# Two FFT convolutions: the transposes between the stages moved from TensorE and PSUM copies to crossbar DMA

## The chip, the cores and the metric

The kernel runs on one core of one Trainium2 chip. The metric is device time in microseconds (us), the median of several executions; lower is better. A run that is over 1.5% above the fastest of its kernel counts as slow here. A ratio below one means faster than the kernel before. Every ratio is the mean time of one kernel's fast runs over the mean time of the kernel before in the same rounds on the same chip, so it is not quite the ratio of the medians quoted beside it. The bracket after a ratio is its 95% interval.

Engine names in the profile: PE is TensorE's matmuls, PEld its weight loads, DVE is VectorE, ACT is ScalarE, POOL is GpSimd, SPq is the DMA queue that SyncE issues. L222 is a source line. Line numbers differ between kernels because the edits shift them.

## The reference, cut to what matters

Four residual layers over a sequence of 2048 rows by 512 features, in bfloat16:

```python
x = A_u
x = x + A(layernorm(x))   # long convolution, by FFT
x = x + B(layernorm(x))   # dilated sliding attention, window 8, 32 heads
x = x + A(layernorm(x))   # the same convolution kernel again
x = x + B(layernorm(x))

def A(u):                 # cut
    K  = einsum("dn,dnl,dn->dl", Cc, exp(logdA * l), dB).real   # kernel of 2048 taps per feature
    Yf = rfft(pad(u)) * rfft(pad(K))
    return irfft(Yf)[:L] + u * Dskip
```

The first layer must also make K, from tables of powers, and its spectrum. The third layer re-uses the spectrum, which the first has stored in DRAM.

## The kernel before

An FFT of each block of features has two stages, each a matmul with constants. Stage 1 (`s1`) gives `Z`, stage 2 (`s2`) needs `Z` with its two axes exchanged, `zt`. In the kernel before, TensorE transposes eight 128x128 blocks into PSUM and VectorE or ScalarE copies them out.

```python
def s2(self, Z, cs, dsts, what):                 # cut
    def turn(i):
        pt = self.psT.tile([128, 2, 4, 128], BF, name="pt", tag="psT")
        for r in range(2):
            for g in range(4):
                nc.tensor.transpose(pt[:, r, g, :], Z[:, r, i * 4 + g, :], ident[:])
        zt = self.w.tile([128, 2, 512], BF, name="zt", tag="zt")
        self.evac("zt_" + what, zt[:]..., pt[:]...)
        zts[i] = zt
    turn(0)
    for i in range(cs):
        if i + 1 < cs:
            turn(i + 1)
        zt = zts.pop(i)
        xp = self.pst([128, 2, 512])             # from the pool psA
        ... four matmuls with C2, then self.evac(what, dsts[i], xp[:])
```

PSUM holds two pools in the first convolution: `psA`, two buffers of 4 KB per partition for every matmul result, and `psT`, two buffers of 2 KB for the transposes.

```python
psT = es.enter_context(tc.tile_pool(name="k_psT", bufs=2, space=PSUM))
psA = es.enter_context(tc.tile_pool(name="k_psA", bufs=2, space=PSUM))
cv = Conv(nc, tc, es, C, X, psA, psT, ("zt_xc",))
```

The first convolution works on four blocks of 128 features while VectorE makes the tables for the next ones (`Xtab`, `Ytab`, `Y2tab`). After the last table comes an end that has no tables left to fill gaps: two halves of a last 64 features (u = 0, 1) get their spectrum, a product, an inverse and the final matmuls. Their spectra have a function of their own. It uses `psT` for the transposes and for the results `xpu`.

```python
def spectrum32(self, KT, drow, dst, ps):         # cut: stage 1 into psu, copied to Z by two engines
    pt = self.psT.tile([128, 2, 4, 128], BF, name="pt", tag="psT")
    zt = self.w.tile([128, 2, 512], BF, name="zt", tag="zt")
    ... eight transposes, two copies
    for r, (a, b) in ((0, (0, 2)), (1, (1, 0))):
        xp = self.psT.tile([128, 512], F32, name="xpu", tag="psT")
        nc.tensor.matmul(xp[:], C2[:, a, :], zt[:, 0, :], start=True, stop=False)
        nc.tensor.matmul(xp[:], C2[:, b, :], zt[:, 1, :], start=False, stop=True)
        (nc.scalar.copy if r == 0 else nc.vector.tensor_copy)(dst[:, r, :], xp[:])
```

The second convolution is a software pipeline over 16 chunks, with a lag for each stage:

```python
for k in range(16 + 13):
    for fn, lag in ((final, 13), (inverse, 8), (product, 7), (s2, 6), (turn, 5), (s1, 0)):
        if 0 <= k - lag < 16:
            fn(k - lag)
```

A build step orders each engine's instructions by the program's order, its priorities and the free buffers. The order is then fixed, and an instruction that is ready can stand behind one that waits; a case, at 247.47 us, is shown below.

## Time and profile before

608.52 us, median of 3 runs (607.86 to 608.82).

The first line is the page's part 1: busy time, share of the span, instructions. After it comes the table of stretches for the middle of the first convolution (72 to 115 and 115 to 233.4 us), its end (233.4 to 268) and the second convolution (398 to 468): length, busy time of each engine, the granted clock of TensorE as a share, the share of DMA time, GB/s.

```profile
PE 445.1 (73%) x5743; PEld 289.0 (48%) x5786; DVE 514.4 (85%) x976; ACT 338.9 (56%) x465; POOL 12.7 (2%) x50
...
72.00:115.00 43.00, 30.98 (x737) 21.24 (x741) 41.14 (x75) 25.30 (x27) 0.83 (x6) 0.91 0.08 26
115.00:233.40 118.40, 85.36 (x1805) 63.44 (x1814) 112.03 (x212) 65.15 (x81) 0.72 (x6) 0.89 0.21 64
233.40:268.00 34.60, 22.81 (x362) 16.35 (x364) 27.37 (x88) 19.49 (x31) 6.06 (x1) 0.80 0.34 107
398.00:468.00 70.00, 57.35 (x571) 42.52 (x576) 63.06 (x141) 49.17 (x66) 0.00 (x0) 0.95 0.00 1
```

VectorE is busy 41.1 of 43 us and 112.0 of 118.4 us in the middle of the first convolution, and 63.1 of 70 us in the second: it sets the time there. At the end of the first convolution it is busy 27.4 of 34.6 us only; a chain through all engines runs there.

The next lines are VectorE's timeline in the second convolution: start, duration, engine and line, what it wrote from what. One period of the pipeline:

```profile
410.54 0.68 DVE L726 TENSOR_TENSOR pa<-xc,Kt 128x1024 bf16<-128x1024 bf16 x1
411.14 0.68 DVE L727 TENSOR_TENSOR pb<-xc,Kt 128x1024 bf16<-128x1024 bf16 x1
411.74 0.69 DVE L708 COPY zt<-pt 128x1024 bf16<-128x1024 bf16 x1
412.34 0.68 DVE L749 CAST VT<-vp 128x512 bf16<-128x512 f32 x1
412.94 0.42 DVE L728 TENSOR_TENSOR Y<-pa,pb 128x512 bf16<-128x512 bf16 x1
413.27 0.42 DVE L729 TENSOR_TENSOR Y<-pa,pb 128x512 bf16<-128x512 bf16 x1
413.61 0.69 DVE L726 TENSOR_TENSOR pa<-xc,Kt 128x1024 bf16<-128x1024 bf16 x1
```

From `pa` to the next `pa` is 3.07 us with no gap. The `zt` copy takes 0.60 us of it from start to start (its duration of 0.69 overlaps the next instruction). It is what the change would remove.

### The profile page before, as it was taken

Reading aid. Unit: us, or ns where it says so; the run is one execution under the profiler, and the core shown is the slowest. Engines: PE = TensorE matmul, PEld = TensorE weight load, DVE = VectorE, ACT = ScalarE, POOL = GpSimd, SP = SyncE. Lnnn points to the kernel's source line nnn. Section 1 sums busy time; section 2 is a strip of 40 time slices with the busy share of each in tenths; the row PEclk is TensorE's granted clock in tenths of the full one; section 3 lists DMA queues with packets and bytes.
Section 4 is the critical chain, followed back from the end, with each engine's and each line's share of the span. In section 5 each row is a group of like instructions: output and inputs, shape, how many; then the busy total and the mean of one; then the engine's idle time right before and its main releaser. Section 6 shows DMA issues by size and latency. Waiting matters only on the chain.

```text
span 606.0 us, 13365 instructions
## 1 busy us (share of the span) xinstructions
PE 445.1 (73%) x5743; PEld 289.0 (48%) x5786; DVE 514.4 (85%) x976; ACT 338.9 (56%) x465; POOL 12.7 (2%) x50
## 2 busy tenths in 40 slices
PE   1101776876767776679987779978995899858996
PEld 0100554564554565454332766656764433327763
DVE  5999799998998999775977899859999588689950
ACT  4999357555662755646574223467973556722144
POOL 0000000000000000400000000000000000000000
PEclk9999989898996897869998599989998799968999
DMA  9101001221131023600004060000000000040011
GB/s 291 67 1 35 19 20 37 87 56 36 41 103 37 3 106 72 209 1 1 2 1 118 4 264 16 2 0 1 3 1 0 2 2 0 1 121 1 1 72 69
DMA packets 24346, 28.78 MB, mean 47 GB/s; under 512 B 15074, under 2 KB 20067, under 8 KB 23007
## 3 DMA queue, kind: packets, MB, share of 16 engines
q1 hardware_dynamic: 22702, 27.54, 13.8%
q8 instruction: 45, 0.74, 0.5%
q10 hardware_dynamic: 1584, 0.39, 0.3%
q14 instruction: 15, 0.11, 0.1%
HBM read 15.89 MB, written 8.39 MB: 40 GB/s over the span
## 4 chain that ended last, share of the span: by engine, by line
DVE 52%; PE 28%; ACT 9%; issue 8%; DMA 2%; POOL 0%; SPq 0%; POOLq 0%; ACTq 0%; DVEq 0%
PE ps_qk L829 7%; DVE prod L931 6%; DVE ta L479 4%; DVE Y2tab L518 4%; DVE tb L480 4%; DVE Ytab L516 4%; PE ps_o L955 4%; PE ps_v L843 3%; DVE Xtab L481 3%; DVE ln_st_b L150 3%; PE Lp L875 2%; DVE Ytab L481 2%; PE po L946 2%; DVE ln_st_a L150 2%; DVE pa L726 2%
## 5 line engine op out<-in xcount | busy, mean ns | idle before, releaser
L946 PE MATMUL po<-sb_ident,prod 128*128 128x128 bf16 x1024 | 72.7, 232 | 11.4 <-DVE prod L931 7.9
L946 PEld LDWEIGHTS <-prod 128*128 128x128 bf16 x1024 | 65.2, 105 | 20.6 <-DVE prod L931 17.2
L829 PE MATMUL ps_qk<-xnT,wqk 128*128 128x512 bf16 x245 | 63.7, 391 | 4.3 <-ACT xnT L814 1.2
L862 DVE TENSOR_TENSOR prod<-qT,kT 128x2048 bf16<-128x2048 bf16 (+3 forms) x48 | 43.2, 953 | 14.0 <-ACT qT L831 7.2
L931 DVE TENSOR_TENSOR prod<-V,L 128x2048 bf16<-128x2048 bf16 (+3 forms) x48 | 43.6, 947 | 6.4 <-PE po L946 6.4
L949 ACT CAST oT<-po 128x1024 bf16<-128x1024 f32 x16 | 15.4, 1015 | 56.6 <-PE po L946 56.6
L195 PE MATMUL psA<-X,sb_F 128*128 128x128 bf16 x128 | 14.9, 236 | 36.2 <-ACT X L578 32.3
L870 DVE TENSOR_TENSOR prod<-qT,kT 128x2048 bf16<-128x2048 bf16 (+3 forms) x40 | 34.9, 902 | 6.9 <-ACT kT L831 4.3
L829 PEld LDWEIGHTS <-wqk 128*128 128x128 bf16 x256 | 23.5, 100 | 32.5 <-issue 12.2
L195 PEld LDWEIGHTS <-sb_F 128*128 128x128 bf16 x256 | 16.6, 100 | 45.6 <-issue 42.8
L535 PE MATMUL psk<-Ytab,Xtab 128*32 128x64 bf16 x1024 | 26.1, 214 | 15.6 <-DVE Xtab L481 5.8
L955 PE MATMUL ps_o<-wo_t,oT 128*128 128x512 bf16 x121 | 33.5, 380 | 4.7 <-ACT oT L949 3.9
L931 DVE TENSOR_TENSOR prod<-Vp,L 128x2048 bf16<-128x2048 bf16 (+3 forms) x40 | 34.9, 896 | 0.0
L182 ACT CAST Z<-psA 128x1024 bf16<-128x1024 f32 (+1 forms) x32 | 28.8, 974 | 9.6 <-PE psA L195 9.5
L875 PE MATMUL Lp<-prod,sb_bones 128*32 128x512 bf16 x256 | 25.4, 416 | 9.6 <-DVE prod L870 4.9
L538 PE MATMUL psk<-Y2tab,Xtab 128*32 128x48 bf16 x1024 | 24.8, 211 | 9.8 <-issue 7.3
L535 PEld LDWEIGHTS <-Xtab 128*32 128x32 bf16 x1024 | 22.7, 113 | 17.9 <-issue 15.2
L516 DVE TENSOR_TENSOR Ytab<-Ytab,MA 128x2048 bf16<-128x2048 bf16 (+1 forms) x33 | 30.6, 929 | 0.2
L518 DVE TENSOR_TENSOR Y2tab<-Ytab,MB 128x2048 bf16<-128x2048 bf16 (+1 forms) x33 | 30.6, 927 | 0.0
L843 PE MATMUL ps_v<-wv,xnT 128*128 128x512 bf16 x126 | 28.2, 379 | 1.8 <-ACT V L845 1.7
L538 PEld LDWEIGHTS <-Xtab 128*32 128x32 bf16 x1024 | 22.2, 106 | 13.0 <-issue 11.8
L150 DVE BATCH_NORM_STATS2 ln_st_b<-X 128x6 f32<-128x384 bf16 (+2 forms) x80 | 23.5, 357 | 3.8 <-ACT X L308 3.8
(195 smaller groups left out, 1100.0 us busy)
## 6 DMA issues: line engine op xcount, KB each, us to landing
kt_scratch<-Kt SPq DMA_DIRECT2D x4, 1024.0 KB, 4.3
Kt<-kt_scratch SPq DMA_DIRECT2D x4, 1024.0 KB, 7.2
Vp<-V SPq DMA_DIRECT2D x2, 1568.0 KB, 9.1
X<-in_A_u_dram SPq DMA_DIRECT2D x4, 512.0 KB, 5.6
Xr<-in_A_u_dram SPq DMA_DIRECT2D x4, 512.0 KB, 4.6
out_dram<-X SPq DMA_DIRECT2D x4, 512.0 KB, 2.6
k_scratch<-KTq SPq DMA_DIRECT2D x7, 256.0 KB, 2.0
KT<-k_scratch SPq DMA_DIRECT2D x7, 256.0 KB, 3.5
```

The source lines that it names most:

```text
L150: self.nc.vector.bn_stats(self.st[:, j, part, :], X[:, j, a:b])
L516: nc.vector.tensor_tensor(v(Y[:, :, :, q * EYB:(q + 1) * EYB, :]), src, vm(self.mult(self.MA, lev, hc, EYB)), ALU.mult)
L518: nc.vector.tensor_tensor(v(Y2[:, :, :, (q - 1) * EYB:q * EYB, :]), src, vm(self.mult(self.MB, lev, hc, EYB)), ALU.mult)
L535: nc.tensor.matmul(psk[32 * g:32 * g + 32, ds, :], xs, Y[:, m // 2, h, :, t], start=(m == 0), stop=False, skip_group_check=True)
L538: nc.tensor.matmul(psk[32 * g:32 * g + 32, ds, EYB:], xs, Y2[:, 1 - m // 2, h, :, t], start=False, stop=(m == 3), skip_group_check=True)
L829: nc.tensor.matmul(ps[:], wqk[:, ct, f0:f0 + 128], xnT[:, ct, s0:s0 + 512], start=(ct == 0), stop=(ct == 3))
L843: nc.tensor.matmul(ps[:].rearrange("p a b -> p (a b)"), xnT[:, ct, j * 128:(j + 1) * 128], wv[:, ct, :], start=(ct == 0), stop=(ct == 3))
L862: nc.vector.tensor_tensor(pr[:, :, (ja - j0) * 128:(ja - j0) * 128 + n], qT[fp][:, :, ja * 128: ja * 128 + n], kT[fp][:, :, (ja - sh) * 12 ...
L875: nc.tensor.matmul(Lp[r0:r0 + 32, w // 4, :], bones[:, w % 4, :], pr[:, f2, hb * 512:(hb + 1) * 512], start=(w % 4 == 0), stop=(w % 4 == 3 ...
L931: nc.vector.tensor_tensor(p2[:, ja - j0: ja - j0 + n, :].rearrange("p j (t d h) -> p (j t) d h", t=2, d=DH), src.rearrange("p j (t d h) -> ...
L946: nc.tensor.matmul(po[f2][:, jj, :], p2[:, jj, f2 * 128:(f2 + 1) * 128], ident[:], start=(w == 0 and jj % 4 == 0), stop=(w == W - 1), skip ...
L955: nc.tensor.matmul(ps[:], oT[:, ft, j * 128:(j + 1) * 128], wo_t[:, ft, :], start=(ft == 0), stop=False)
```

## The change

The intent: take 384 transposes from TensorE and their copies from VectorE and ScalarE, and let the DMA crossbar do them from SBUF to SBUF, in 46 transfers of 256 KB and 4 of 128 KB. The PSUM of `psT` becomes a third `psA` buffer (a fourth in the second convolution). The Trainium skill, page "DMA: Bandwidth & Descriptors", section "DMA Transpose (X-bar)", says that plain transfers of this kind are issued from the Sync or Scalar queue only, and, under its heading on two transposing streams, that two streams in flight together can corrupt each other. The change puts all of them on one queue.

```diff
+def turn(nc, zt, Z, g0, n):
+    for r in range(2):
+        nc.sync.dma_start_transpose(zt[:, r, 0:n * 128].rearrange("q (g k) -> q g k", k=128),
+                                    Z[:, r, g0:g0 + n, :].rearrange("k g q -> k (g q)"))
 ... in s2:
-        def turn(i):  (transposes into psT, copy out)
+        for i0 in range(0, cs, 2):
+            zt = self.w.tile([128, 2, 1024], BF, name="zt", tag="zt")
+            turn(nc, zt, Z, i0 * 4, 8)
+            for i in range(2):
+                zts[i0 + i] = zt[:, :, i * 512:i * 512 + 512]
 ... in spectrum32:
-        pt = self.psT.tile(...)  (transposes, two copies)
+        zt = self.w.tile([128, 2, 1024], BF, name="zt", tag="zt")
+        turn(nc, zt, Z, 0, 4)
+        xp = self.pst([128, 2, 512])
         for r, (a, b) in ((0, (0, 2)), (1, (1, 0))):
-            xp = self.psT.tile([128, 512], F32, name="xpu", tag="psT")
-            ... matmuls into xp[:]
+            ... matmuls into xp[:, r, :], copied out by ScalarE (r = 0) and VectorE (r = 1)
 ... first convolution:
-        psT = es.enter_context(tc.tile_pool(name="k_psT", bufs=2, space=PSUM))
-        psA = es.enter_context(tc.tile_pool(name="k_psA", bufs=2, space=PSUM))
+        psA = es.enter_context(tc.tile_pool(name="k_psA", bufs=3, space=PSUM))
 ... second convolution:
-        psA ... bufs=3   psT ... bufs=2
+        tp = es.enter_context(tc.tile_pool(name="a_zt", bufs=2))
+        psA ... bufs=4
-        def turn(k):   (eight transposes, VectorE copy)
+        def turns(k):
+            if k % 2 == 0:
+                t = tp.tile([128, 2, 1024], BF, name="zt", tag="zt")
+                turn(nc, t, Z[k // 4], (k % 4) * 4, 8)
+                zt[k], zt[k + 1] = t[:, :, 0:512], t[:, :, 512:1024]
```

To make room in SBUF, one constant (`bones`) and one set of statistics are also allocated later; that moves a small load and is left aside.

More of the change, by code (lines that the diff above doesn't have):

```diff
@@ L90, in make_consts @@
     fc = _fft_consts()
-    bones_np = np.zeros((128, 4, 32), dtype=np.float32)
-    for f in range(128):
-        for k in range(4):
-            bones_np[f, k, 8 * k + f // 16] = 1.0
     for name in ("F1", "F1T"):
@@ L97, in make_consts @@
     todo = [("ident", _bf(np.eye(128)), BF), ("C2", _bf(fc["C2"]), BF), ("IC", _bf(fc["IC"]), BF),
-            ("bones", _bf(bones_np), BF), ("onesr", _bf(np.ones((1, 128))), BF)]
+            ("onesr", _bf(np.ones((1, 128))), BF)]
     for i, (name, arr, dt) in enumerate(todo):
@@ L117, in load_x, with load_b_weights @@
     return X
-def load_b_weights(nc, const, wqkv, wo):
+def load_b_weights(nc, const, C, wqkv, wo):
+    bones_np = np.zeros((128, 4, 32), dtype=np.float32)
+    for f in range(128):
+        for k in range(4):
+            bones_np[f, k, 8 * k + f // 16] = 1.0
+    C["bones"] = const.tile([128, 4, 32], BF, name="sb_bones")
     wqk = const.tile([128, 4, 1024], BF, name="wqk")
@@ L130, in load_b_weights @@
         nc.sync.dma_start(wo_t[:, ft, :], src)
+    nc.sync.dma_start(C["bones"][:], nc.inline_tensor(_bf(bones_np), name="c_bones").ap())
     Vp = const.tile([128, 2, NJ - 2, 256], BF, name="Vp")
@@ L161, in norm, with __init__ @@
         self.nc.vector.tensor_scalar(dst, src, self.rstd[:, j:j + 1], self.nb[:, j:j + 1], ALU.mult, ALU.add)
+def turn(nc, zt, Z, g0, n):
+    for r in range(2):
+        nc.sync.dma_start_transpose(zt[:, r, 0:n * 128].rearrange("q (g k) -> q g k", k=128),
+                                    Z[:, r, g0:g0 + n, :].rearrange("k g q -> k (g q)"))
 class Conv:
-    def __init__(self, nc, tc, es, C, X, psA, psT, on_dve, zbufs=2, pbufs=2, vbufs=1):
-        self.nc, self.C, self.X, self.psA, self.psT, self.on_dve = nc, C, X, psA, psT, on_dve
+    def __init__(self, nc, tc, es, C, X, psA, on_dve, zbufs=2, pbufs=2, vbufs=1):
+        self.nc, self.C, self.X, self.psA, self.on_dve = nc, C, X, psA, on_dve
         self.vbufs = vbufs
@@ L201, in s2 @@
     def s2(self, Z, cs, dsts, what):
-        nc, ident, C2 = self.nc, self.C["ident"], self.C["C2"]
+        nc, C2 = self.nc, self.C["C2"]
         zts = {}
-        def turn(i):
-            pt = self.psT.tile([128, 2, 4, 128], BF, name="pt", tag="psT")
-            for r in range(2):
-                for g in range(4):
-                    nc.tensor.transpose(pt[:, r, g, :], Z[:, r, i * 4 + g, :], ident[:])
-            zt = self.w.tile([128, 2, 512], BF, name="zt", tag="zt")
-            self.evac("zt_" + what, zt[:].rearrange("q r k -> q (r k)"), pt[:].rearrange("q r g k -> q (r g k)"))
-            zts[i] = zt
-        turn(0)
+        for i0 in range(0, cs, 2):
[3 more added lines that the diff above has]
+                zts[i0 + i] = zt[:, :, i * 512:i * 512 + 512]
         for i in range(cs):
-            if i + 1 < cs:
-                turn(i + 1)
             zt = zts.pop(i)
@@ L313, in spectrum32 @@
     def spectrum32(self, KT, drow, dst, ps):
-        nc, F1, C2, ident = self.nc, self.C["F1"], self.C["C2"], self.C["ident"]
+        nc, F1, C2 = self.nc, self.C["F1"], self.C["C2"]
         Z = self.z.tile([128, 2, 16, 128], BF, name="Z", tag="Z")
@@ L326, in spectrum32 @@
             (nc.scalar.copy if jh == 0 else nc.vector.tensor_copy)(Z[:, :, 0:4, sl], ps[:, :, :, sl])
-        pt = self.psT.tile([128, 2, 4, 128], BF, name="pt", tag="psT")
-        zt = self.w.tile([128, 2, 512], BF, name="zt", tag="zt")
-        for r in range(2):
-            for g in range(4):
-                nc.tensor.transpose(pt[:, r, g, :], Z[:, r, g, :], ident[:])
-            (nc.vector.tensor_copy if r == 0 else nc.scalar.copy)(zt[:, r, :], pt[:, r].rearrange("q g k -> q (g k)"))
+        zt = self.w.tile([128, 2, 1024], BF, name="zt", tag="zt")
+        turn(nc, zt, Z, 0, 4)
+        xp = self.pst([128, 2, 512])
         for r, (a, b) in ((0, (0, 2)), (1, (1, 0))):
-            xp = self.psT.tile([128, 512], F32, name="xpu", tag="psT")
-            nc.tensor.matmul(xp[:], C2[:, a, :], zt[:, 0, :], start=True, stop=False)
-            nc.tensor.matmul(xp[:], C2[:, b, :], zt[:, 1, :], start=False, stop=True)
-            (nc.scalar.copy if r == 0 else nc.vector.tensor_copy)(dst[:, r, :], xp[:])
+            nc.tensor.matmul(xp[:, r, :], C2[:, a, :], zt[:, 0, 0:512], start=True, stop=False)
+            nc.tensor.matmul(xp[:, r, :], C2[:, b, :], zt[:, 1, 0:512], start=False, stop=True)
+            (nc.scalar.copy if r == 0 else nc.vector.tensor_copy)(dst[:, r, :], xp[:, r, :])
 def load_params(nc, pp, prm):
@@ L580, in kernel_and_first_conv @@
             ladder(nc, pp, pst, identf, raw, MA, MB, cb, nu, fill)
-        psT = es.enter_context(tc.tile_pool(name="k_psT", bufs=2, space=PSUM))
-        psA = es.enter_context(tc.tile_pool(name="k_psA", bufs=2, space=PSUM))
-        cv = Conv(nc, tc, es, C, X, psA, psT, ("zt_xc",))
+        psA = es.enter_context(tc.tile_pool(name="k_psA", bufs=3, space=PSUM))
+        cv = Conv(nc, tc, es, C, X, psA, ())
         kp = es.enter_context(tc.tile_pool(name="k_kt", bufs=1))
@@ L677, in a_layer @@
         wk = es.enter_context(tc.tile_pool(name="a_wk", bufs=3))
-        psA = es.enter_context(tc.tile_pool(name="a_psA", bufs=3, space=PSUM))
-        psT = es.enter_context(tc.tile_pool(name="a_psT", bufs=2, space=PSUM))
+        tp = es.enter_context(tc.tile_pool(name="a_zt", bufs=2))
+        psA = es.enter_context(tc.tile_pool(name="a_psA", bufs=4, space=PSUM))
         ident, C2, IC, F1, F1T = C["ident"], C["C2"], C["IC"], C["F1"], C["F1T"]
@@ L699, in s1 @@
             nc.scalar.copy(Z[dc][:, :, :, q * 32:(q + 1) * 32], ps[:])
-        def turn(k):
-            dc, c = k // 4, k % 4
-            pt = psT.tile([128, 2, 4, 128], BF, name="pt", tag="psT")
-            for r in range(2):
-                for g in range(4):
-                    nc.tensor.transpose(pt[:, r, g, :], Z[dc][:, r, c * 4 + g, :], ident[:])
-            zt[k] = wk.tile([128, 2, 512], BF, name="zt", tag="zt")
-            nc.vector.tensor_copy(zt[k][:].rearrange("q r k -> q (r k)"), pt[:].rearrange("q r g k -> q (r g k)"))
+        def turns(k):
[3 more added lines that the diff above has]
+                zt[k], zt[k + 1] = t[:, :, 0:512], t[:, :, 512:1024]
         def s2(k):
@@ L768, in a_layer @@
         for k in range(16 + 13):
-            for fn, lag in ((final, 13), (inverse, 8), (product, 7), (s2, 6), (turn, 5), (s1, 0)):
+            for fn, lag in ((final, 13), (inverse, 8), (product, 7), (s2, 6), (turns, 5), (s1, 0)):
                 if 0 <= k - lag < 16:
@@ L1011 @@
     ln_b = LnStats(nc, const, [(0, 3 * DCH), (3 * DCH, D - 64), (D - 64, D)], "b", eps)
-    ln_b2 = LnStats(nc, const, [(0, 3 * DCH), (3 * DCH, D)], "b2", eps)
     X, marks = kernel_and_first_conv(nc, tc, C, prm, A_u[0], const, kt_dram, kscr, ln, ln_b)
     const2 = ctx.enter_context(tc.tile_pool(name="const2", bufs=1))
-    Wt, Vp = load_b_weights(nc, const2, B_wqkv, B_wo)
+    ln_b2 = LnStats(nc, const2, [(0, 3 * DCH), (3 * DCH, D)], "b2", eps)
+    Wt, Vp = load_b_weights(nc, const2, C, B_wqkv, B_wo)
     marks = b_layer(nc, tc, C, X, Wt, Vp, ln_b, marks, ln_next=ln)
```

## The prediction

> **What bounds the kernel now.** The page shows VectorE busy 85% of a 606.0 us span, and 52% of the chain that ended last. Both convolutions are bound by VectorE. First convolution with the kernel tables (45 to 266 us): in the table of stretches VectorE is busy 95 to 98% of most 25 us slices up to 190 us, TensorE 60 to 80%. Second convolution (398 to 467 us): in the chain, in order of time, VectorE runs a period of 3.06 us per block: pa 0.60, pb 0.60, the zt copy 0.60, VT 0.60, Y 0.33 twice.
>
> **What goes.** TensorE: 384 transposes, about 0.11 us apart when streamed, some 42 us. VectorE: zt copies 16 x 0.684 us (first) and 16 x 0.682 us (second), in sequence about 0.60 us each, so 9.6 to 11 us per convolution, plus two 0.42 us copies. ScalarE: 14 copies of 1.02 us, mostly off the path. The freed PSUM gives the matmuls one buffer more.
>
> **What comes.** 46 transposing DMAs of 256 KB and 4 of 128 KB, all in order on one queue: 30 full ones in the first convolution, 16 in the second. The trace has none such. Plain 256 KB loads land 3.2 us after issue; 512 KB in 256-byte pieces 4.5 us. The Trainium skill, page "DMA: Bandwidth & Descriptors", section "Latency and other measured facts", gives 261 GB/s for a transposing DMA with a non-contiguous middle dimension; the page "VectorE: DVE Perf Modes", section "The three transpose paths", gives 1309 ns for one 128x128 block. These bracket 1.0 us to 10 us for eight blocks. My estimate, from the first figure and the plain loads: 2.5 us of queue time and 4.5 us to landing.
>
> **On the critical path.**
> - First convolution, 72 to 200 us: the copies stand in VectorE's own sequence, so about 10 us go; the forward transforms have slack, but TensorE, in order, will sometimes stand at a late zt. Net -7 us.
> - Its end, 197 to 262 us: transposes of the last spectra (243 to 250 us) stand in a chain with little filler; a DMA landing replaces about 1.5 us of transposes and copy. Net +4 us.
> - Second convolution: first product 3 us later; then 16 periods shrink from 3.06 to about 2.6 us (VectorE 2.46; ScalarE about 2.6 where Z, xc and VT overlap). If a DMA takes over 2.5 us of queue time, the DMAs set the period instead. Net -3 us.
> - Attention layers: unchanged.
>
> Sum -6 us less some 1.5 us for waits in the DMA queue: **604 us**, 8 in 10 between **588** and **650**. Chances: faster by over 2% **0.27**, within 2% **0.40**, slower by over 2% **0.33**.
>
> **What would show it.** VectorE busy falls from 514 to about 492 us, TensorE from 445 to about 405, ScalarE from 339 to about 324. The DMA issues show zt<-Z, 256 KB, landing in 3 to 6 us. The second convolution's period is about 2.6 us; its first product comes about 3 us later after the first stage. "TensorE matmul psA/xp waits for DMA zt" appears among the waits, below 20 us in all. The end of the first convolution lengthens.
>
> **What would make it wrong.** Slower: a transposing DMA holds the queue for over 4 us each (16 of them are then over 64 us in a 60 us stage, and 30 of them over 120 us), so both convolutions become bound by DMA; or transposes queue behind stores that wait for ScalarE (the queue already waits 128 us for KTq). Faster: landings of about 3 us, always hidden, give -16 us or better, near 590.

## More of the kernel before

VectorE's waits in the end of the first convolution (233 to 265 us): what waited, on what, us in total, times, the longest.

```profile
DVE ln_st_b L150 <- ACT X L308: 3.8, 2, 2.5
DVE VT L277 <- ACT VT L275: 1.5, 1, 1.5
DVE Z L326 <- PE psu L322: 1.3, 1, 1.3
DVE Kt L337 <- PE xpu L336: 0.4, 1, 0.4
```

These are 7.0 us in all, by adding the four.

## The result, and the profile after

607.41 us, median of 4 runs (605.50 to 607.84); the kernel before 608.67 us, median of 4. The ratio is 0.9976 [0.9952, 0.9999]: the same within 2%, a gain of 0.24% where the prediction had 0.75% (4.5 us of 608.5). The result is correct.

The same views as before: part 1, and the table of stretches.

```profile
PE 422.6 (70%) x5362; PEld 261.7 (43%) x5402; DVE 497.0 (82%) x942; ACT 323.0 (53%) x449; POOL 12.9 (2%) x50
...
72.00:115.00 43.00, 26.79 (x613) 15.84 (x617) 38.50 (x68) 18.25 (x19) 0.68 (x4) 0.70 0.59 98
115.00:233.40 118.40, 78.65 (x1821) 55.94 (x1828) 111.96 (x211) 59.46 (x76) 0.70 (x6) 0.86 0.50 104
233.40:268.00 34.60, 19.77 (x179) 11.30 (x177) 15.73 (x56) 14.67 (x24) 6.06 (x1) 0.65 0.45 118
398.00:468.00 70.00, 55.69 (x476) 37.72 (x480) 57.85 (x132) 50.69 (x72) 0.00 (x0) 0.93 0.31 61
```

VectorE lost 17.4 us of work, TensorE 22.5, ScalarE 15.9. In the third stretch VectorE, ScalarE and TensorE are less busy than before. Part of this is only that the end now starts 8 us earlier. Measured from the last table to the first transposes of attention (233.4 to 264.8 us before, 225.1 to 268.3 after), VectorE has the same work, 24.2 and 23.8 us, in 31.4 and in 43.2 us. That is where to look.

To see it, follow milestones through the timelines. Both profiled executions have a span of 606.0 us, so the stages must cancel. The differences in the last column are subtractions.

| stage, from one milestone to the next | before | after | difference |
|---|---|---|---|
| start to the last `Y2tab` instruction (middle of the first convolution) | 233.4 | 225.1 | -8.3 |
| to the first transpose `pt_x` of attention 1 (end of the first convolution) | 31.4 | 43.2 | +11.8 |
| to the first copy of Z in the second convolution (attention 1) | 133.0 | 135.0 | +2.0 |
| to the first normalised row `xn` of attention 2 (second convolution) | 69.6 | 65.0 | -4.6 |
| to the end (attention 2) | 138.6 | 137.7 | -0.9 |

These are single executions; runs of one kernel here differ by up to about 7 us (`e9_tail_dma_pools` below, 592.90 to 600.16), so a difference of one or two microseconds in one row proves nothing.

The transfers, in the view of the tile `zt`: the time that the issuing instruction held its queue (least, median and most, in ns) and the time from issue to landing.

```profile
L169 SPq DMA_TRANSPOSE zt<-Z x50: 1189/1308/2332, 69.7 to 444.9; - x50
...
  DMA zt<-Z: 24.2, 13
...
DMA to landing us min/median/max: 2.5/3.3/6.2
```

One transfer holds the queue 1.31 us and lands after 3.3 us; the prediction had 2.5 and 4.5. TensorE waited 24.2 us for `zt` in all, in 13 places. The same view puts 19.3 us of it (14.4 and 4.9) on stage-2 matmuls of the first convolution, where VectorE sets the time and TensorE has slack.

One period of the second convolution on VectorE:

```profile
430.69 0.69 DVE L719 TENSOR_TENSOR pa<-xc,Kt 128x1024 bf16<-128x1024 bf16 x1
431.30 0.68 DVE L720 TENSOR_TENSOR pb<-xc,Kt 128x1024 bf16<-128x1024 bf16 x1
432.02 0.42 DVE L721 TENSOR_TENSOR Y<-pa,pb 128x512 bf16<-128x512 bf16 x1
432.37 0.42 DVE L722 TENSOR_TENSOR Y<-pa,pb 128x512 bf16<-128x512 bf16 x1
432.70 0.69 DVE L742 CAST VT<-vp 128x512 bf16<-128x512 f32 x1
433.73 0.69 DVE L719 TENSOR_TENSOR pa<-xc,Kt 128x1024 bf16<-128x1024 bf16 x1 [0.35 <-ACT xc L711]
```

The `zt` copy is gone. The period shown is 3.04 us, not 2.47; 0.35 us of the difference is a wait for ScalarE's `xc`, the rest lies in small gaps between starts. It is the longest of the 15 but for the last: their median is 2.66 us (3.15 before) and their mean 2.80 (3.23 before). ScalarE is near its own limit there: its timeline has `xc`, `Z`, `X` and `VT` back to back in 2.85 us (432.69 to 435.54). From the first `pa` to the first `xn` it is 53.2 us instead of 59.4 (from the two timelines), 0.39 us per chunk. What it pays is at the start: the first product waits 8.8 us in place of 1.6.

VectorE's waits at the end of the first convolution (225 to 268 us):

```profile
DVE ln_st_b L152 <- ACT X L309: 8.6, 2, 7.3
DVE Z L327 <- issue: 3.0, 1, 3.0
DVE pa L266 <- ACT Kt L334: 2.4, 1, 2.4
DVE VT L278 <- ACT VT L276: 2.4, 1, 2.4
DVE pa L266 <- ACT Kt L191: 1.6, 1, 1.6
DVE y L285 <- PE psA L292: 0.8, 1, 0.8
DVE Kt L334 <- PE psA L333: 0.4, 1, 0.4
```

They add up to 19.2 us, 12.2 more than before, and so account for the +11.8. The largest wait is for ScalarE's final result X. TensorE's timeline of these microseconds shows what stands behind it (the bracket is the idle time before the instruction and what ended it):

```profile
232.87 0.19 PE L323 MATMUL psu<-KTu,sb_F 128*128 128x32 bf16 x1 [4.37 <-DMA KTu<-k_scratch]
...
246.75 0.39 PE L305 MATMUL psA<-VT,sb_F1T 128*128 128x64 bf16 x8 [1.16 <-ACT VT L276]
...
247.44 0.19 PE L305 MATMUL psA<-VT,sb_F1T 128*128 128x64 bf16 x1
247.47 0.38 PE L332 MATMUL psA<-zt,sb_C 128*128 128x512 bf16 x1
247.68 0.38 PE L333 MATMUL psA<-zt,sb_C 128*128 128x512 bf16 x1
...
251.70 0.38 PE L332 MATMUL psA<-zt,sb_C 128*128 128x512 bf16 x1 [2.98 <-ACT Kt L334]
```

L332 is the first matmul of the last spectrum. Its transposes were issued at 236.63 us and the queue was done with them at 239.13; with the median landing they were there by about 241 (estimate: the second was issued near 237.9, plus the 3.3 us above). But in TensorE's fixed order L332 stands behind inverse and final matmuls (L305) of an earlier part, and starts at 247.47, 14.6 us after the spectrum's first matmul `psu` at 232.87. In the kernel before the first one on record came 7.9 us after it (238.5 to 246.41). A smaller part of the +11.8 lies before `psu`: from the last table to `psu` it is 7.8 us, 5.1 before, and TensorE stands 4.37 us of it at the fetch of `KTu` (the first line above), for which it did not stand before. From `psu` to `pt_x` it is 35.4 us, 26.3 before. Then the second half of the same PSUM tile waits 2.98 us for the copy of the first. ScalarE, meanwhile, stands at two copies of a weight, `wv`, whose load was issued behind the transposes; the chain of waits (start, us on the chain, engine) passes through it:

```profile
243.88 4.60 DMA wvn<-in_B_wqkv_dram
248.57 2.11 ACT wv L831 x2
250.68 0.49 ACT X L309
251.34 0.38 DVE ln_st_b L152 x3
```

### The profile page after: what moved, and what is told of

The parts are those of the page before. It is cut to its first block, busy times and chain, and to the rows that moved or that the text cites. A ratio compares the mean times of both kernels' runs of the same rounds, so it can differ in the third digit from the quotient of the medians.

```text
span 606.0 us, 12631 instructions
## 1 busy us (share of the span) xinstructions
PE 422.6 (70%) x5362; PEld 261.7 (43%) x5402; DVE 497.0 (82%) x942; ACT 323.0 (53%) x449; POOL 12.9 (2%) x50
## 4 chain that ended last, share of the span: by engine, by line
PE 27%; DVE 21%; ACT 9%; issue 7%; DMA 2%; POOL 0%; SPq 0%; POOLq 0%; ACTq 0%
PE ps_qk L822 7%; DVE prod L924 6%; PE ps_o L948 4%; PE ps_v L836 3%; PE Lp L868 2%; PE pt_x L802 2%; PE po L939 2%; DVE prod L863 1%; DVE ln_st_b L152 1%; ACT xc L711 1%; DVE pa L719 1%; DMA zt<-Z 1%; DVE pb L720 1%; ACT oT L942 1%; PE ps_o L950 1%
## 5 line engine op out<-in xcount | busy, mean ns | idle before, releaser
L939 PE MATMUL po<-sb_ident,prod 128*128 128x128 bf16 x1024 | 70.4, 227 | 13.7 <-DVE prod L924 10.3
L939 PEld LDWEIGHTS <-prod 128*128 128x128 bf16 x1024 | 62.3, 102 | 23.5 <-DVE prod L924 20.1
L855 DVE TENSOR_TENSOR prod<-qT,kT 128x2048 bf16<-128x2048 bf16 (+3 forms) x48 | 43.2, 953 | 14.0 <-ACT qT L824 7.2
L822 PEld LDWEIGHTS <-wqk 128*128 128x128 bf16 x256 | 23.4, 100 | 32.1 <-issue 11.8
L204 PEld LDWEIGHTS <-sb_F 128*128 128x128 bf16 x256 | 17.4, 106 | 42.6 <-issue 40.0
L532 PE MATMUL psk<-Ytab,Xtab 128*32 128x64 bf16 x1024 | 23.7, 206 | 12.9 <-DVE Ytab L513 5.6
L535 PE MATMUL psk<-Y2tab,Xtab 128*32 128x48 bf16 x1024 | 22.8, 202 | 13.5 <-issue 12.2
L868 PE MATMUL Lp<-prod,sb_bones 128*32 128x512 bf16 x256 | 24.9, 410 | 10.1 <-DVE prod L863 5.1
L532 PEld LDWEIGHTS <-Xtab 128*32 128x32 bf16 x1024 | 20.9, 105 | 17.8 <-issue 15.5
L222 PE MATMUL psA<-zt,sb_C 128*128 128x512 bf16 x30 | 15.6, 548 | 18.6 <-DMA zt<-Z 14.4
```

Source lines behind the costliest of these rows:

```text
L204: nc.tensor.matmul(o, F1[:, j, r, :], rhs_j(j), start=True, stop=not dk)
L532: nc.tensor.matmul(psk[32 * g:32 * g + 32, ds, :], xs, Y[:, m // 2, h, :, t], start=(m == 0), stop=False, skip_group_check=True)
L822: nc.tensor.matmul(ps[:], wqk[:, ct, f0:f0 + 128], xnT[:, ct, s0:s0 + 512], start=(ct == 0), stop=(ct == 3))
L855: nc.vector.tensor_tensor(pr[:, :, (ja - j0) * 128:(ja - j0) * 128 + n], qT[fp][:, :, ja * 128: ja * 128 + n], kT[fp][:, :, (ja - sh) * 12 ...
L868: nc.tensor.matmul(Lp[r0:r0 + 32, w // 4, :], bones[:, w % 4, :], pr[:, f2, hb * 512:(hb + 1) * 512], start=(w % 4 == 0), stop=(w % 4 == 3 ...
L939: nc.tensor.matmul(po[f2][:, jj, :], p2[:, jj, f2 * 128:(f2 + 1) * 128], ident[:], start=(w == 0 and jj % 4 == 0), stop=(w == W - 1), skip ...
```

## The experiments

Four theories for the +11.8 us at the end:

- **D, the DMA itself**: a landing of about 3.3 us twice, in a chain with no filler, where TensorE and a copy needed some 1.5 us by the prediction's count.
- **P, PSUM**: the change also moved the spectrum's results from a pool of their own (`psT`) into the pool that inverse and final matmuls use. The wait is for a free buffer and for the order that follows, not for the transpose.
- **H, the half tile**: only the one tile of two halves matters, whose second half waits for the copy of the first.
- **L, the loads**: the weights of attention are late behind the transposes in the same queue, and ScalarE stands at `wv`.

All outputs are right.

### Each convolution alone

`e1_conv2_only` keeps the kernel before in the first convolution; `e2_conv1_only` keeps it in the second.

```diff
 e1_conv2_only, against the change
-        psA ... bufs=3;  s2 and spectrum32 by turn() on the DMA
+        psT ... bufs=2, psA ... bufs=2;  s2 and spectrum32 by nc.tensor.transpose and copies
 e2_conv1_only, against the change
-        for fn, lag in (..., (turns, 5), (s1, 0)):       # DMA, psA bufs=4
+        for fn, lag in (..., (turn, 5), (s1, 0)):        # TensorE and VectorE, psA bufs=3, psT bufs=2
```

> Only the second convolution uses the transposing DMA; the first is as in the kernel before (the loads of the weights still moved as in the change). In the two traces the stretch from the end of the first attention layer's last output matmul to the first transposes of the second attention layer shrinks by about 4 us. Theory (the second convolution gains, the end of the first one loses what its middle gains): about 604.5 us, 4 us below the kernel before (ratio 0.993). Rival (both convolutions gain little, the DMA eats its own gain everywhere): 608 us, ratio 0.999.

> Only the first convolution uses the transposing DMA. Theory: its middle gains 8 us, its end loses 12 us, so it is about 3 to 4 us slower than the kernel before: 612 us, ratio 1.006. Rival: the two effects cancel everywhere, ratio 0.999.

Measured: `e1_conv2_only` 605.00 us, ratio 0.9947 [0.9929, 0.9965]; `e2_conv1_only` 613.59 us, ratio 1.0085 [1.0066, 1.0104]; the kernel before 607.75 us (11 runs). The second convolution is a gain of about 0.5% by itself, and the first a loss of about 0.9%. In the trace of `e2_conv1_only` the end of the first convolution is again long, 225.4 to 268.8 us. The two effects do not add up to the change: multiplied, the ratios give 1.0032, and the change measured 0.9976. About 3 us of this sum have no explanation here.

### The end on TensorE, and the half tile

`e3_tail_pe` gives the last spectra back to TensorE with a `psT` pool, which leaves `psA` two buffers for the whole first convolution. `e4_two_xp` changes nothing but the half tile: two tiles from the shared pool.

```diff
 e3_tail_pe
-        turn(nc, zt, Z, 0, 4)                    # in spectrum32
+        ... eight nc.tensor.transpose into psT, two copies; xpu from psT, as in the kernel before
-        psA = es.enter_context(tc.tile_pool(name="k_psA", bufs=3, space=PSUM))
+        psT = es.enter_context(tc.tile_pool(name="k_psT", bufs=2, space=PSUM))
+        psA = es.enter_context(tc.tile_pool(name="k_psA", bufs=2, space=PSUM))
 e4_two_xp
-        xp = self.pst([128, 2, 512])
         for r, (a, b) in ((0, (0, 2)), (1, (1, 0))):
+            xp = self.pst([128, 512])
```

> The change, but the last two spectra of 32 channels (the end of the first convolution) are transposed by TensorE again, with their two separate PSUM tiles, and PSUM of the first convolution is divided as before (2 + 2 buffers). Theory (the loss of 12 us lies in this end): 8 of the 12 us or more come back: 598 to 600 us against 607.4 of the change. The first VectorE table of the end still ends 8 us earlier than in the kernel before. Rival (the loss comes from the weight loads queued behind transposes and from the KTu fetch, not from these transposes): at most 3 us come back, 604 to 607 us.

> The change, but in the last two spectra the two halves of the result have two PSUM tiles again instead of one of two halves; the transposes stay on the DMA. Theory (in the change the second half's matmuls wait until ScalarE has evacuated the first half, 3.0 and 1.2 us in the trace): 3 to 4 us faster than the change, 603.5 to 604.5 us. Rival (the wait only shifts to the DMA or to ScalarE, which is held by the weight copies): within 1 us of the change.

Measured: `e3_tail_pe` 613.51 us, ratio 1.0092 [1.0070, 1.0115], a clear miss. `e4_two_xp` 606.71 us, ratio 0.9973 [0.9955, 0.9991], as the change: theory H falls.

The miss of `e3_tail_pe` has a cause in its trace. The last table now starts at 220.0 us, 5 us earlier than in the change, but the products of the third block come after it (first `pa` at 220.73) instead of amid the tables (214.71 in the change). From `psu` to `pt_x` the end took 25.5 us, 35.4 in the change and 26.3 before. So the end was mended and the middle spoilt: with two `psA` buffers the build made another order. The experiment had changed two things.

### The pool of the middle and the pool of the end apart

`e5_tail_pe_pools` keeps three `psA` buffers through the middle, then closes that pool and opens `psT` (2) and `psA` (2) in its place. In size it is the same PSUM: 3 x 4 KB is 2 x 4 KB + 2 x 2 KB. The last spectra are on TensorE. `e6_ps2` is the change with two `psA` buffers and nothing else. `e7_loads_pool` sends the weight loads through GpSimd's queue, and `e8_tail_pe_pools_loads` does both.

```diff
 e5_tail_pe_pools
-        psA = es.enter_context(tc.tile_pool(name="k_psA", bufs=3, space=PSUM))
+        es_main = es.enter_context(ExitStack())
+        psA = es_main.enter_context(tc.tile_pool(name="k_psA", bufs=3, space=PSUM))
 ... before the end of the first convolution:
+        es_main.close()
+        cv.psT = es.enter_context(tc.tile_pool(name="k_psT", bufs=2, space=PSUM))
+        cv.psA = es.enter_context(tc.tile_pool(name="k_psA2", bufs=2, space=PSUM))
 ... and spectrum32 as in e3_tail_pe
 e6_ps2
-        psA = es.enter_context(tc.tile_pool(name="k_psA", bufs=3, space=PSUM))
+        psA = es.enter_context(tc.tile_pool(name="k_psA", bufs=2, space=PSUM))
 e7_loads_pool (and e8_tail_pe_pools_loads, on top of e5_tail_pe_pools)
-    nc.sync.dma_start(wqk[:], wsrc[:, :, 0:1024])
+    nc.gpsimd.dma_start(wqk[:], wsrc[:, :, 0:1024])     # wvn, wo_t and bones likewise
```

> The clean form of the previous try with the end on TensorE: the middle of the first convolution keeps the change's three PSUM buffers, and only for the end they are given back as 2 + 2, so that VectorE's order of work up to the end is that of the change, and the last two spectra are transposed by TensorE into separate tiles as before. Theory (the change loses 12 us at this end): the end's stretch, from the last Y2tab table to the first transposes of the attention layer, falls from 42.8 us (change) to 31 to 34 us; in all 597 to 600 us, ratio 0.985. Rival (the end is long because it starts 8 us too early for its inputs: the KTu fetch, the weight loads): stretch 38 us or more, in all 603 us or more.

> The change with two instead of three PSUM buffers in the first convolution [...]; all transposes on the DMA. If the previous try with the end on TensorE (613.5 us) was slow only because two buffers make the build order the products of the third block after the last table, this one is slow too: the products come after the last Y2tab, in all 617 to 622 us. Rival (that try was slow because of the end itself): about 608 us.

> The change, with the attention weights loaded from GpSimd's queue instead of the queue of the transposes. Theory (weight copies on ScalarE wait for wvn, which waits behind two transposes that wait for Z; ScalarE then holds X and the first half of the last spectra; VectorE stands 7.3 us): the wait of VectorE for X falls from 7.3 to 3 to 5 us, in all 603 to 605 us. Rival (the order of TensorE, not the loads, holds the spectra): within 1 us of the change.

> Both edits: the end on TensorE with its PSUM given back, and the weights from GpSimd's queue. If the two are separate causes: 1 to 3 us below the end on TensorE alone, 595 to 599 us, ratio 0.98. If the loads only hurt through the DMA transposes at the end: equal to the end on TensorE alone within 1 us.

| kernel | median us | ratio | last `Y2tab` | first `pt_x` |
|---|---|---|---|---|
| before (11 runs) | 608.08 | 1 | | |
| `e5_tail_pe_pools` | 599.52 | 0.9862 [0.9848, 0.9876] | 223.7 | 258.9 |
| `e6_ps2` | 617.00 | 1.0162 [1.0139, 1.0186] | 218.1 | 279.3 |
| `e7_loads_pool` | 605.54 | 0.9955 [0.9943, 0.9967] | 222.9 | 264.4 |
| `e8_tail_pe_pools_loads` | 600.71 | 0.9877 [0.9857, 0.9897] | | |

`e5_tail_pe_pools` gains some 7 us on the change, as expected. `e6_ps2` shows that the third buffer is worth having (it is missing there at the end too): two buffers make the tables end earlier and everything else later, the same other order as in `e3_tail_pe`. VectorE's waits in its trace (200 to 280 us), the two largest:

```profile
DVE ln_st_b L152 <- ACT X L309: 12.2, 3, 5.9
DVE pa L266 <- ACT Kt L191: 8.8, 3, 4.6
```

The loads explain little. `e7_loads_pool` took ScalarE's wait for the load of `wv` away, and VectorE's largest wait moved to the next link, as its waits (225 to 265 us) show:

```profile
DVE pa L266 <- ACT Kt L334: 8.2, 2, 6.4
```

`Kt` L334 is the copy of the spectrum's result, whose matmul stands behind the final matmuls here too (245.61 us, 15.5 after `psu`). ScalarE's three copies of `wv` (244.14 us, 3.15 us) also still stand before it in ScalarE's order, so this run moves the load and not the copies. Once PSUM is parted, moving the loads adds nothing: `e8_tail_pe_pools_loads` and `e5_tail_pe_pools` have overlapping intervals. Theory L is worth about 2 us at most, and only while P stands; by the ratios it is 1.3 us on the change, with intervals that overlap.

### PSUM or DMA

`e5_tail_pe_pools` still changed two things, the pools and the path of the transposes. `e9_tail_dma_pools` parts PSUM in the same way but leaves the last spectra on the DMA, so it parts P from D. `e10_mix_first` adds to `e5_tail_pe_pools` the remedy for the second convolution's late start: the first pair of chunks is transposed by TensorE and VectorE. `e11_half_dma` halves the size of each transfer and doubles the number, to see what a transfer costs the queue.

```diff
 e9_tail_dma_pools: pools as in e5_tail_pe_pools, and in spectrum32
         turn(nc, zt, Z, 0, 4)
-        xp = self.pst([128, 2, 512])
         for r, (a, b) in ((0, (0, 2)), (1, (1, 0))):
+            xp = self.psT.tile([128, 512], F32, name="xpu", tag="psT")
 e10_mix_first, in the second convolution
+                if k == 0:
+                    for i in range(2):
+                        pt = psA.tile([128, 2, 4, 128], BF, name="pt", tag="psA")
+                        ... eight nc.tensor.transpose from Z[0], then
+                        nc.vector.tensor_copy(t[:, :, i * 512:i * 512 + 512], ...)
+                else:
                     turn(nc, t, Z[k // 4], (k % 4) * 4, 8)
 e11_half_dma, on top of e5_tail_pe_pools, in turn()
+    m = n // 2
+    for h in range(2):
         for r in range(2):
             ... the same transfer for m blocks from g0 + h * m
```

> As the good try (PSUM given back as 2 + 2 for the end, the last spectra's results in two tiles of the small pool), but the last two spectra are transposed by the DMA, as in the change. This parts the two things that the good try undid together. Theory P (the loss of the end came from the spectra sharing the large PSUM buffers, so that TensorE got them only after the third block's outputs): 600 to 602.5 us, near the good try's 599.5. Theory L (the loss came from the landing of the DMA, 2.5 to 5.0 us there, in a chain without filler): 604.5 us or more, near the change's 607.4.

> The good try, and the first pair of blocks of the second convolution transposed by TensorE and VectorE, the other seven pairs by the DMA. The trace shows 11.9 us from the first Z to the first product with the DMA and 10.3 us with TensorE. Theory (this start is paid in full): 1 to 1.5 us below the good try. Rival (VectorE's two copies of 0.68 us and the PSUM buffers they take eat it): within 0.7 us of the good try.

> The good try with every transposing DMA cut into two of half the size: 92 DMAs of 128 KB for 46 of 256 KB, so the queue's issue time doubles to about 1.25 us x 4 = 5 us per pair of blocks, while the first block of a pair can land as early as before. Theory (the queue has room: 16 x 1.3 us in a 60 us stage): the second convolution's 32 issues take 40 us of 60 and the middle of the first 5 us more per chunk, mostly hidden; 599.5 to 603 us. Rival (the queue was near its limit): over 606 us.

Measured, against 607.82 us before (11 runs): `e9_tail_dma_pools` 597.48 us (592.90 to 600.16, 6 runs), ratio 0.9820 [0.9791, 0.9849]; `e10_mix_first` 596.85 us, ratio 0.9819 [0.9806, 0.9831]; `e11_half_dma` 623.77 us, ratio 1.0269 [1.0244, 1.0295].

`e9_tail_dma_pools` decides it. It has the change's transposes at the end, on the same queue, and is some 10 us faster than the change, at no loss against `e5_tail_pe_pools`. VectorE's waits at its end (225 to 259 us), the largest three, and TensorE's spectrum matmuls there:

```profile
DVE Kt L334 <- PE xpu L333: 3.3, 2, 3.0
DVE ln_st_b L152 <- ACT X L309: 1.8, 2, 1.0
DVE Z L327 <- issue: 1.8, 1, 1.8
...
232.78 0.18 PE L323 MATMUL psu<-KTu,sb_F 128*128 128x32 bf16 x1 [3.04 <-DMA KTu<-k_scratch]
...
238.56 0.59 PE L332 MATMUL xpu<-zt,sb_C 128*128 128x512 bf16 x2 [0.83 <-DMA zt<-Z]
239.87 0.59 PE L333 MATMUL xpu<-zt,sb_C 128*128 128x512 bf16 x2 [0.71 <-DMA zt<-Z]
...
246.68 0.61 PE L332 MATMUL xpu<-zt,sb_C 128*128 128x512 bf16 x1 [1.84 <-DMA zt<-Z]
```

The first spectrum matmul now follows `psu` (232.78 us in its trace) by 5.8 us, not 14.6. It waits for the DMA, but for 0.83 us; the second half waits 1.84 us. The end lasts 33.1 us (225.8 to 258.9), 1.7 us more than before and 10.1 us less than in the change. From `psu` to `pt_x` it is 26.1 us, as long as before (26.3); the 1.7 us lie before `psu`, at `KTu`. The landing of the DMA thus costs nothing here that the traces show, and the division of PSUM most of the +11.8. The other traces say the same: with the pools parted the end took 35.2, 38.2 and 34.6 us with TensorE's transposes (`e5_tail_pe_pools`, `e8_tail_pe_pools_loads`, `e10_mix_first`), and 33.1 and 34.7 with the DMA (this run and `e12_best` below); with the pools shared, 41.5 to 43.4 (the change, `e2_conv1_only`, `e4_two_xp`, `e7_loads_pool`).

Two limits. Parting the pools changes three things together: where the results lie, the number of `psA` buffers at the end (three to two), and the point at which one pool is closed and the others are opened. Which of them moved the spectrum forward in TensorE's order was not tested. And the granted clock of the end differs: 0.78 before, 0.70 in the change, 0.90 in this trace, with TensorE busy 20.8, 23.1 and 18.8 us. By these busy times the clock could carry some 2 us of the +11.8 and 4 of the 10.1 (an estimate); in `e12_best`, at 0.75, the end was 34.7 us.

The Trainium skill, page "Perfetto Trace Analysis", section "Optimization Strategy", says that a gap repeating on the engine that should be saturated can mean that PSUM or SBUF lacks room for the next tile. This is a relative of that and not the sign itself: of the 12.2 us of added waits on VectorE, 9.8 went away with another division of the same bytes (all its waits there add up to 9.4 us, 19.2 in the change), but they were single waits in a chain, and no wait named PSUM; the releaser shown was ScalarE's copy.

`e10_mix_first` lies below `e5_tail_pe_pools` by 0.0043 in the ratio, about 2.6 us. They were run at other times. In its trace the wait of the first product for `xc` is 2.62 us, and 8.77 us in that of `e5_tail_pe_pools`.

`e11_half_dma` shows that a transfer of half the size costs the queue almost as much. In the queue's timeline (start, us, instruction, count) eight of 128 KB take

```profile
110.62 12.47 SPq L171 DMA_TRANSPOSE zt<-Z  x8
```

Their median is 1267 ns against 1308 ns for 256 KB, and the landing is 2.5 us. Eight smaller ones for a chunk of features take 10 to 12.5 us in place of 5.4 to 7.1 us for four. The tables then end at 247.3 us, 23.6 us later than in `e5_tail_pe_pools`: TensorE waits 31.8 us for `zt` in this stage (16.1 and 15.7 us in its two largest groups), 18.7 in `e5_tail_pe_pools`, and VectorE, which sets the time there, waits 28.7 us in place of 5.3, by adding its waits, mostly for TensorE's results. The second convolution did not suffer: 65.5 us, 65.0 in the change, although its 32 transfers held the queue from 421.5 to 465 us almost without a gap.

### The best version, and larger transfers

`e12_best` is `e9_tail_dma_pools` with the first pair of `e10_mix_first`. `e13_whole_dma` is `e9_tail_dma_pools` with transfers of 512 KB, two for a chunk, and for want of SBUF only one `zt` buffer in the first convolution.

```diff
 e13_whole_dma
-        for i0 in range(0, cs, 2):
-            zt = self.w.tile([128, 2, 1024], BF, name="zt", tag="zt")
-            turn(nc, zt, Z, i0 * 4, 8)
+        zt = self.w.tile([128, 2, 2048], BF, name="zt", tag="zt")       # pool f_w: bufs=1
+        turn(nc, zt, Z, 0, cs * 4)
 ... and in the second convolution turn(nc, t, Z[k // 4], 0, 16) at every fourth k
```

> The two edits that helped, together: PSUM given back as 2 + 2 for the end with the last spectra still transposed by the DMA, and the first pair of the second convolution transposed by TensorE. If they are separate: 1 to 2.5 us below the former alone (597.5), so 594.5 to 596.5 us, ratio 0.979. If the one hides the other: 597 us or more.

> PSUM given back as 2 + 2 for the end, and each chunk of 128 channels transposed by two DMAs of 512 KB instead of four of 256 KB (one zt buffer of twice the size in the first convolution, two in the second). Cutting the DMAs in half cost 24 us. Theory I (what costs is the issue, about 1.3 us each whatever the size): each 512 KB DMA is issued in 1.3 to 1.6 us, the middle of the first convolution, to the last Y2tab, is 0 to 3 us shorter, in all 595 to 598 us. Theory B (the queue's time goes with the bytes): 2.5 us or more per issue, no gain or 600 us and more, since the first block of a chunk now waits for the whole chunk.

Measured, against 608.79 us before (11 runs): `e12_best` 595.73 us (591.14 to 597.47, 6 runs), ratio 0.9784 [0.9751, 0.9817]; `e13_whole_dma` 616.89 us, ratio 1.0138 [1.0110, 1.0166].

`e12_best` beats both kernels; whether by more than 2% its interval leaves open. The next two lines are the first product of the second convolution in VectorE's timeline, of the change and then of `e12_best`:

```profile
415.18 0.69 DVE L719 TENSOR_TENSOR pa<-xc,Kt 128x1024 bf16<-128x1024 bf16 x1 [8.84 <-ACT xc L711]
```

```profile
397.99 0.69 DVE L731 TENSOR_TENSOR pa<-xc,Kt 128x1024 bf16<-128x1024 bf16 x1 [1.56 <-ACT xc L723]
```

From the first copy of Z to that product it is 8.7 us, against 11.9 in the change and 10.3 before; the whole second convolution takes 62.9 us, against 65.0 and 69.6. That is some 2.5 us below `e9_tail_dma_pools` (65.4), whose interval overlaps; the rest of the distance between these two traces lies in the first convolution, where their code is the same, and is taken for scatter.

In `e13_whole_dma` a 512 KB transfer holds the queue 2.56 us in the first convolution (median of 14) and 1.77 us in the second (of 8), and lands after 5.1 and 3.9 us. Its slowness cannot be laid to the size: its tables ended early, at 220.6 us, with the products after them, the order of `e3_tail_pe` and `e6_ps2`, although it has three `psA` buffers in the middle. TensorE waited 27.5 us for `zt` there (60 to 226 us), 21.4 in `e9_tail_dma_pools`. Whether larger transfers with two buffers would help is open.

## Why the prediction was right or wrong, point by point

- **"First convolution, 72 to 200 us … Net -7 us"**: right. The last table started 8.3 us earlier.
- **"Its end, 197 to 262 us … a DMA landing replaces about 1.5 us of transposes and copy. Net +4 us"**: this is the step that failed. The end became 11.8 us longer. The place was right, and so was its direction; the term was too small by 8 us, and its cause was another. The landing is not it: in `e9_tail_dma_pools`, with the DMA kept, the end was 33.1 us against 31.4 before, and equal from `psu` on. Nor had the old path been as short as 1.5 us: from the first transpose to the first spectrum matmul on record it took 3.2 us, with other work between (243.22 to 246.41), and by DMA 2.5 (236.11 to 238.56). What the prediction had left out was the order. With the spectrum's results in the shared PSUM pool, its first matmul stood behind others and came 14.6 us after `psu`; with the pools parted it came after 5.8, and 10.1 us came back (8.5 in `e12_best`).
- **"The freed PSUM gives the matmuls one buffer more"**: right for the middle: taking it away cost 1.86% of the time (the ratios 1.0162 and 0.9976), though that run had it away at the end too. It was counted as free. At the end the same exchange took a separate pool away from the chain, and the prediction did not ask who else had lived in `psT`.
- **"Second convolution: first product 3 us later; then 16 periods shrink from 3.06 to about 2.6 us … Net -3 us"**: right in sum. The product came 1.6 us later after the first stage, the chunks shrank by 0.39 us on average, and the stage lost 4.6 us; the stage alone measured 0.9947. The periods are near the 2.6 us: 2.66 in the median, 2.80 on the mean, the longest ones with waits for ScalarE, whose copies of `X` the prediction had not counted.
- **"2.5 us of queue time and 4.5 us to landing"**: too high. 1.31 and 3.3 us were measured, within the 3 to 6 us given as a sign. The feared queue limit of 2.5 us per chunk did not appear in the change. With transfers of half the size the first convolution's middle suffered, and the second convolution still did not.
- **"Sum -6 us less some 1.5 us for waits in the DMA queue"**: no such term shows by itself. The nearest is the late `wvn` load, worth about 2 us (`e7_loads_pool`) while PSUM was shared.
- **"Attention layers: unchanged"**: +2.0 and -0.9 us in the two traces, no more than single executions scatter.
- **"VectorE busy falls from 514 to about 492 us, TensorE from 445 to about 405, ScalarE from 339 to about 324"**: 497.0, 422.6, 323.0. VectorE's copies were worth 0.60 us each in sequence, not 0.68, so 32 of them and two of 0.33 make 19.9 us (estimate from the timeline before); why 17.4 went is not explained. TensorE lost its 381 instructions, but its stage-2 matmuls became longer: the L222 group 548 ns on the mean, the matching group 446 before. The granted clock from 72 to 115 us was 0.70 in this trace, 0.91 before; in that of `e9_tail_dma_pools`, with the same DMAs, it is 0.86, and the L222 group is as long there, 546 ns. Neither is explained.
- **"waits for DMA zt, below 20 us in all"**: 24.2 us by the view of the tile, a near miss and without weight, since 19.3 us of it lie where VectorE sets the time.
- **The predicted time**: 604.0 us with 588 to 650; 607.41 lies inside, and "within 2%" was given the best chance. The change of 4.5 us was 1.3 us, by the medians of its own rounds. That the total came so near is partly luck. By the two traces the end lost 7.8 us more than predicted, while the middle and the second convolution gained 2.9 us more, and the predicted 1.5 us of queue waits did not show.

What stays open: some 3 us by which the two halves of the change do not add up; the lower granted clock; which part of the parted pools does it; why the build chooses the other order with two buffers (the traces show the order and its price, not the reason); larger transfers with two buffers.

## What to carry to other kernels

When a change frees a resource, ask who used its other half: here a pool that held transposes also kept the results of a latency-bound chain out of a crowded pool, and losing it cost most of what the removed copies had won (8.5 to 10.1 of some 13 us). Give the throughput-bound middle and the latency-bound end different pools, even in the same bytes; closing one pool and opening two won 1.6% over the change (ratios 0.9820 and 0.9976). Mix the paths: crossbar DMA where the pipeline is full, and the short way over TensorE for the first chunks, for which everything waits; that was worth some 2 us.

## What the Trainium skill lacked or had wrong

- "VectorE: DVE Perf Modes", section "The three transpose paths": it gives 1309 ns for one 128x128 block by the DMA crossbar. Eight blocks in one transfer held the queue 1.31 us and landed after 3.3 us (median of 50), four blocks 1.27 us and 2.5 us, so the figure does not multiply with the number of blocks; the page does not say whether it is queue time or time to landing.
- "DMA: Bandwidth & Descriptors", section "Latency and other measured facts": it gives 261 GB/s for transposing transfers with a non-contiguous middle dimension, and this section has no queue time by size. Here the queue was held 1.27 us for 128 KB, 1.31 for 256 KB, and 2.56 and 1.77 for 512 KB (medians in the first and the second convolution). Worked out from these that is 103, 200, and 205 to 296 GB/s: nearly a fixed cost up to 256 KB, and the page's figure is reached only at 512 KB.
- "TensorE: Matmul & The Clock Gate", section "Part 4: PE-mode transpose": about 390 ns in isolation and about 275 ns in one kernel. In the kernel before, the three groups of FFT transposes (384 in all, view of the tile `pt`) have medians of 218 to 219 ns.
- No page was found that says that the way PSUM is divided into pools can set an instruction's place in an engine's order. Here that was worth about 10 us of 606 (43.2 against 33.1 us at the end of the first convolution, 34.7 in a second kernel with the same end).
